# Two weight loads of a two-layer decode kernel are split unevenly over the DMA engines, head 29's keys are kept and loaded in another cut, and the small tasks move behind the values

## The chip, the core and the metric

The kernel runs on one core of a Trainium2 chip. TensorE (PE in the profile) multiplies matrices, VectorE (DVE), ScalarE (ACT) and GpSimd (POOL) work on vectors, SyncE (SP) issues transfers, and sixteen DMA engines move data from the chip's memory into the core's on-chip memory of 128 partitions. SP, ACT and POOL can each issue DMAs. The metric is the device time of one execution in microseconds, as the median of several runs: 1347.92 us before the change (three runs, 1347.71 to 1348.05).

## The reference

Two attention blocks and two MLP blocks run in turn over one token, and the two attention blocks use the same cache and the same weights, as the two MLP blocks do.

```python
def _A_ref(x, k_cache, v_cache, wq, wo):      # x: 1 x 1 x 640, caches: 32 heads x 8192 x 128
    q = heads of (x @ wq)
    scores = einsum("bhqd,bhkd->bhqk", q, k_cache) * (128 ** -0.5)
    p = softmax(scores)
    o = einsum("bhqk,bhkd->bhqd", p, v_cache)
    return o @ wo
def _B_ref(x, w1, w2):                        # 640 -> 1728 -> 640
    return relu(x @ w1) @ w2

x = A_x
x = x + _A_ref(_layernorm(x), A_k_cache, A_v_cache, A_wq, A_wo)
x = x + _B_ref(_layernorm(x), B_w1, B_w2)
x = x + _A_ref(_layernorm(x), ...)            # the same caches and weights again
x = x + _B_ref(_layernorm(x), ...)
```

All data are float32. The keys and values of one head are 8.39 MB, those of all heads 268 MB. They don't fit on the chip, so most of them are read twice, once in each layer.

## The kernel before

**The order of the work.** Layer 0 takes the heads from 0 to 31 and layer 1 from 31 to 0, so that what lies on the chip at the turn is used again. `kept` names the units that stay: the last units of head 29, the last of head 30 and all of head 31. Sizes are counted in places; a place is 8 floats in each of the 128 partitions, which is 4,096 bytes over all of them. `KEPT` is the number of places that stay, 3960 before the change. Keys and values go into one buffer, `ring`, of `KEPT + 800` places.

**Loads.** `todo` is the list of all loads in their order. `pump` (line 210) takes the first one, looks for a free place for it (`place`, or a fixed slot for the heads 2 to 26, which are called `FULL`) and issues it on SP's queue (line 230). If there is no room it returns and tries again at the next `release`, which follows the matmuls that read a piece (`scores`, line 509; `values`, line 564). A load of the ring has one row in each of the 128 partitions, so each of the sixteen engines carries eight rows of it, and the load has landed when the last of the sixteen has done its rows. The heads 27 to 31 are cut into units (`UNITS`), and each unit is one load. At the turn three loads go beside the ring, into `mix` and `wct` (`load_beside`, line 240), as soon as the tiles are free, and a `None` in `todo` holds SP until then. The program gives the DMAs that SP and ACT issue eight completion semaphores in turn; a DMA is issued when the one that had its semaphore eight DMAs before has landed.

**Weights.** The query weights and the output weights come in groups of four heads. A group is 10,240 bytes in a partition. They go into `pair` and are issued by ACT (`load_wq` line 278, `load_pair` lines 284 and 288). In layer 1 the second group's query weights are issued at the layer's start (line 729) and first read by `queries_by_halves` (line 434) beside the second head. Twelve of W2's fourteen row blocks come through the ring at the end of each layer; the last two (`w2_t`, `F_REST`) are loaded once, in layer 0 by ACT (line 809), as 128 rows of 5,120 bytes. Only 64 rows of the second of these blocks hold weights; the other 64 are zeros that nothing reads.

**Small tasks.** `chores` and `slow` are queues of generators: the output projection of a group (`run_out`), the next group's queries, and the product of W1 with the last head's output weights (`mixing`, `mixing_quarter`), which is made once in each layer. `side_work` advances them. In the `FULL` heads it runs twice between the exponentials and the values; in the other heads between the pieces of the keys and values. `keep_busy` issues matmuls whose result nobody reads, in layer 1 also beside the values of the last head but one.

**Ends.** A layer's last head (31 in layer 0, 0 in layer 1) comes in small pieces. After its last keys land there follow its scores, exponentials, values, the MLP and the layer's sum; in layer 1 the output is then stored.

Of the kernel before, what the change touches and what calls it, by code (L numbers as in the profile page):

```python
# [105 lines left out]
def decode_kernel(ctx: ExitStack, tc: tile.TileContext, x, kv, wqo, w1, w2, w2_rest, out):  # L106
# [16 lines left out]
    apart = {(29, 9): (3800, KEPT), (30, 0): (4464, 4544), (30, 1): (4544, RING), (30, 2): (3072, 3800)}  # L123
# [4 lines left out]
    def all_of(layer, u):  # L128
        todo.append((layer, u, 0, len(UNITS[u[0]][u[1]][1]), None))
# [8 lines left out]
    def turning(layer, heads, slot):  # L138

        for h in heads:  # L140
            for a, end in parts_of(layer, h):
                while a < end:
                    b = min(end, a + SLOTS - slot)
                    todo.append((layer, (h, 0), a, b, SLOT * slot))
                    slot = (slot + b - a) % SLOTS
                    a = b

    def anywhere(layer, h):
        for a, b in parts_of(layer, h):
            todo.append((layer, (h, 0), a, b, None))  # L150
# [21 lines left out]
    for u in W2_ALL:  # L172
        all_of(1, u)
# [36 lines left out]
    def pump():  # L210
        while todo:
# [17 lines left out]
            o = 8 * sum(ns[:first])  # L229
            nc.sync.dma_start(ring[:, 8 * at : 8 * (at + n)], source[u][:, o : o + 8 * n])  # L230
# [904 lines left out]
```

## Time and profile before

| | |
|---|---|
| median of three runs | 1347.92 us (1347.71 to 1348.05) |
| the profiled execution's own time | 1347.7 us |
| its span, first to last instruction | 1345.6 us |
| PE busy | 816.0 us, 61% of the span |
| DVE busy | 248.2 us, 18% |
| ACT busy | 58.6 us, 4% |
| POOL busy | 2.9 us, ten instructions |
| moved by DMA | 574.17 MB, mean 427 GB/s |
| mean granted TensorE clock | 0.807 |

How it is read: the slices and windows give the busy share of the sixteen DMA engines (1.00 is all of them) and the rate. A share above 1 comes where an engine has two packets under way. The chain of waits goes back from the last instruction to what released it at each step. In the list of waits, "SPq L230 <- X" is time in which SP's queue held a load back until X had happened.

### The profile page before, as it was taken

The numbers are of one execution on the slowest core, as the hardware profiler recorded it, in microseconds if no ns is written. First come the engines' busy times: TensorE is split into PE (matmuls) and PEld (weight loads), VectorE is DVE, ScalarE is ACT, GpSimd is POOL, SyncE is SP. The second block draws the span as 40 slices with busy tenths as digits, with TensorE's granted clock in tenths as the row PEclk, the third lists the DMA queues.
The fourth block names the chain that finished last, engine by engine and source line by source line (L and its number), as shares of the span: only waits on it lengthen the run. The fifth ranks groups of instructions, "written<-read, shape, count | busy, mean of one in ns | idle before, by whom it ended". The sixth has DMA issues, their size and how long they took to land.

```text
span 1345.6 us, 13351 instructions
## 1 busy us (share of the span) xinstructions
PE 816.0 (61%) x5968; PEld 264.3 (20%) x5968; DVE 248.2 (18%) x774; ACT 58.6 (4%) x149; POOL 2.9 (0%) x10
## 2 busy tenths in 40 slices
PE   3454565564655655667688754475456554666778
PEld 1111111111211211112252111111112111211224
DVE  1121111221211211112223211122111111111222
ACT  0000000000000000000000000000000000000000
POOL 0000000000000000000000000000000000000000
PEclk9688677887977977777899767787878788777789
DMA  9999999999999999999999999999999999999997
GB/s 406 437 427 438 429 429 433 428 434 431 442 429 426 434 436 420 440 423 412 423 409 425 432 436 432 428 435 433 433 435 425 425 433 436 429 427 449 416 426 329
DMA packets 22672, 574.17 MB, mean 427 GB/s; under 512 B 2516, under 2 KB 2648, under 8 KB 5592
## 3 DMA queue, kind: packets, MB, share of 16 engines
q1 hardware_dynamic: 19592, 529.84, 91.8%
q10 hardware_dynamic: 3024, 43.50, 7.6%
q8 instruction: 46, 0.75, 0.2%
q14 instruction: 10, 0.08, 0.0%
HBM read 573.33 MB, written 0.00 MB: 426 GB/s over the span
## 4 chain that ended last, share of the span: by engine, by line
DMA 61%; PE 29%; DVE 6%; ACT 1%; issue 1%; another core or an unknown queue 1%; SPq 0%; ACTq 0%; DVEq 0%
DMA ring<-in_kv 60%; PE ps L509 14%; PE outs L564 9%; DVE h_t L520 2%; DVE pt L538 1%; ACT p L534 1%; PE acc L478 1%; DMA pair<-in_wqo 1%; PE pm L525 1%; DVE p L601 1%; PE px L434 1%; PE px L466 1%; PE px L685 1%; DVE pT L540 0%
## 5 line engine op out<-in xcount | busy, mean ns | idle before, releaser
L509 PE MATMUL ps<-ring,spread_q 128*32 128x512 f32 (+3 forms) x2104 | 329.1, 775 | 295.2 <-DMA ring<-in_kv 290.3
L564 PE MATMUL outs<-ring,pT 128*4 128x512 f32 (+1 forms) x2032 | 272.3, 674 | 47.1 <-DVE pT L540 24.0
L509 PEld LDWEIGHTS ps<-ring,spread_q 128*32 128x32 f32 x2104 | 78.5, 138 | 480.2 <-issue 335.4
L520 DVE TENSOR_REDUCE h_t<-ps 128x1 f32<-128x512 f32 x64 | 44.2, 691 | 599.8 <-PE ps L509 599.8
L534 ACT ACTIVATE p<-ps,h_t 128x512 f32<-128x512 f32 x64 | 44.0, 687 | 1222.5 <-DVE h_t L532 1222.5
L564 PEld LDWEIGHTS outs<-ring,pT 128*4 128x4 f32 x2032 | 53.3, 93 | 218.1 <-issue 177.2
L611 PE MATMUL pm<-ones,p 128*128 128x1 f32 x120 | 22.9, 260 | 95.0 <-DVE p L601 95.0
L597 DVE TENSOR_SCALAR p<-outs,ind 128x128 f32<-128x128 f32 x60 | 21.0, 351 | 279.0 <-PE outs L564 279.0
L601 DVE SCALAR_TENSOR_TENSOR p<-outs,ind,p 128x128 f32<-128x128 f32 x180 | 63.1, 351 | 6.4
L538 DVE STREAM_TRANSPOSE pt<-p 128x512 f32<-128x512 f32 x64 | 46.5, 727 | 58.2 <-ACT p L534 58.2
L525 PE MATMUL pm<-row_of,h_t 128*128 128x16 f32 x128 | 25.9, 278 | 49.7 <-DVE h_t L520 48.9
L611 PEld LDWEIGHTS pm<-ones,p 128*128 128x128 f32 x120 | 17.8, 188 | 152.2 <-DVE p L601 150.9
L525 PEld LDWEIGHTS pm<-row_of,h_t 128*128 128x128 f32 x128 | 19.6, 192 | 110.0 <-DVE h_t L520 108.3
L434 PE MATMUL px<-pair,ln_xc 128*32 128x256 f32 x280 | 36.6, 412 | 4.2 <-ACT mix L693 4.2
L685 PE MATMUL px<-w_t,wct 128*128 128x448 f32 (+1 forms) x80 | 35.9, 563 | 1.0 <-ACT wct L678 1.0
L478 PE MATMUL acc<-pair,o_cols 128*32 128x320 f32 x224 | 36.3, 471 | 0.0
L434 PEld LDWEIGHTS px<-pair,ln_xc 128*32 128x32 f32 x280 | 16.3, 117 | 23.2 <-ACT mix L693 8.9
L532 DVE TENSOR_REDUCE h_t<-pm 128x1 f32<-128x16 f32 x64 | 11.2, 174 | 32.6 <-PE pm L525 32.6
L478 PEld LDWEIGHTS acc<-pair,o_cols 128*32 128x32 f32 x224 | 12.9, 118 | 17.4 <-issue 16.6
L685 PEld LDWEIGHTS px<-w_t,wct 128*128 128x128 f32 x80 | 13.5, 193 | 10.2 <-issue 8.6
L540 DVE COPY pT<-pt 128x64 f32<-128x64 f32 x64 | 14.3, 224 | 2.2
L615 DVE COPY o_cols<-pm 128x1 f32<-128x1 f32 x56 | 8.9, 158 | 28.4 <-PE pm L611 28.4
(136 smaller groups left out, 215.4 us busy)
## 6 DMA issues: line engine op xcount, KB each, us to landing
ring<-in_kv SPq DMA_DIRECT2D x24, 4096.0 KB, 32.1
ring<-in_kv SPq DMA_DIRECT2D x11, 6144.0 KB, 33.6
ring<-in_kv SPq DMA_DIRECT2D x31, 2048.0 KB, 30.6
pair<-in_wqo ACTq DMA_DIRECT2D x13, 2560.0 KB, 24.5
ring<-in_kv SPq DMA_DIRECT2D x14, 1024.0 KB, 11.9
ring<-in_w SPq DMA_DIRECT2D x4, 1280.0 KB, 25.9
w_t<-in_w ACTq DMA_DIRECT2D x1, 4320.0 KB, 29.0
ring<-in_kv SPq DMA_DIRECT2D x6, 512.0 KB, 28.3
```

What stands on the lines that cost most here:

```text
L434: nc.tensor.matmul(pq[32 * j : 32 * j + 32, :n], xc[:, c : c + 1].to_broadcast([P, 32]), wq_t[g][:, c, j * n : (j + 1) * n], start=(c == 0 ...
L478: nc.tensor.matmul(acc[32 * half : 32 * half + 32, : 2 * DR], col.to_broadcast([P, 32]), wt[:, 2 * half * DR : 2 * (half + 1) * DR], start ...
L509: nc.tensor.matmul(hd.ps[32 * g : 32 * g + 32, c : c + n], spread_q[:, 3 - r : 35 - r], tile_of[:, at + g * n : at + (g + 1) * n], start=f ...
L520: nc.vector.tensor_reduce(hd.nm, hd.ps, AX.X, ALU.max, negate=True)
L525: nc.tensor.matmul(pt[:, :16], hd.nm.to_broadcast([P, P]), row_of.rearrange("p g r -> p (g r)"), start=True, stop=True,)
L534: nc.scalar.activation(hd.p, hd.ps, AF.Exp, bias=hd.low, scale=1.0, accum_out=hd.l)
L538: nc.vector.transpose(pt, hd.p)
L564: nc.tensor.matmul(hd.out[32 * g : 32 * g + 4, r : r + m].rearrange("p r d -> p (r d)"), hd.pT[:, 4 * i : 4 * i + 4], tile_of[:, v : v + m ...
L597: nc.vector.tensor_scalar(oc[:, 0], hd.out[:, 0], ind[:, :1], 0.0, op0=ALU.mult, op1=ALU.add)
L601: nc.vector.scalar_tensor_tensor(oc[:, r], hd.out[:, r], ind[:, r : r + 1], oc[:, r - 1], op0=ALU.mult, op1=ALU.add,)
L611: nc.tensor.matmul(pt[:, :1], oc[:, 3], ones, start=True, stop=True)
L685: nc.tensor.matmul(pt[:, :n], wct[:, c], w1_t[:, c, f : f + n], start=(c == 0), stop=(c == NB - 1),)
```

## The change

- **Kept keys and the cut of head 29.** The last key piece of head 29 that stays grows from 320 to 416 columns and there is no separate 128-column unit. `KEPT` rises by 48 places to 4008, and the ring with it.
- **Longer loads.** `ENDS` and `STARTS` write out the loads at the end of layer 0 and the start of layer 1, and a load may now cover several units, which lie beside each other in a row in memory (`ROWS`). There are 17 loads in place of 27 for the heads 27 to 31 in layer 0, and 11 in place of 15 in layer 1. In layer 0 all keys of head 29 now come ahead of its values.
- **Half of W2's last rows.** ACT loads only rows 64 to 127 of the first of the two blocks (2,560 bytes each). Rows 0 to 63 of both blocks (5,120 bytes each) come in three loads that GpSimd issues, as 2 x 3, 6 x 7 and 8 x 2 rows. The 64 rows of zeros are no longer loaded.
- **80 rows of a group's query weights.** In layer 1 ACT loads rows 80 to 127 of the second group's query weights, and GpSimd rows 0 to 79 as 2 x 2, 6 x 10 and 8 x 2 rows. For both, the source is padded (`_apart`) so that the outer dimension of a load stays 2, 6 or 8.
- **Small tasks.** In the `FULL` heads the PE steps of the small tasks now run after the values, beside the vector work of the head's output, and the others behind the output. The product with the last head's weights is started at head 8 (its load at head 7) and its quarters at heads 10, 14, 18 and 22. `totals` moves behind a head's output, `queries_by_halves` has one pause fewer, and the three `keep_busy` matmuls beside the last head but one run in layer 0 too.
- **Room.** The identity lies in the ring's tail and is made again in layer 1; several small tiles are merged, and GpSimd's scratch is halved.

```diff
...
@@ -47,13 +47,12 @@
     ("k", K_ALL[:1]),
     ("k", K_ALL[1:2]),
     ("k", [(2, 0, 256)]),
-    ("k", [(2, 256, 256), (3, 128, 64)]),
+    ("k", [(2, 256, 256), (3, 0, 96)]),
     ("v", V_ALL[:1]),
     ("v", V_ALL[1:2]),
-    ("k", [(3, 0, 128)]),
     ("v", V_ALL[2:3]),
     ("v", V_ALL[3:]),
-    ("k", [(3, 192, 320)]),
+    ("k", [(3, 96, 416)]),
 ]
...
@@ -61,12 +60,42 @@
...
 UNITS[31] = HALVES[:2] + LAST
-DROPPED = {29: 9, 30: 2}
-KEPT = 3960
+DROPPED = {29: 8, 30: 2}
+ROWS = [[(h, i) for i in range(len(UNITS[h]))] for h in range(29)]
+ROWS += [[(h, i) for i in range(len(UNITS[h]))] for h in (29, 30, 31)]
+ENDS = [
+    [(27, 0)],
+    [(27, 1)],
+    [(28, 0), (28, 1)],
+    [(28, 2), (28, 3)],
+    ROWS[29][:4],
+    [(29, 8)],
+    ROWS[29][4:8],
+    [(30, 0), (30, 1)],
+    [(30, 2)],
+    [(30, 3)],
+    [(30, 4)],
+] + [[u] for u in ROWS[31]]
+STARTS = [
+    [(29, 0)],
+    [(29, 1)],
+    [(29, 2)],
+    [(29, 3)],
+    ROWS[29][4:6],
+    ROWS[29][6:8],
+    ROWS[28][:2],
+    ROWS[28][2:3],
+    [(28, 3)],
+    [(27, 0)],
+    [(27, 1)],
+]
+KEPT = 4008
 W2_PLACES = 800
+W2_SPREAD = [(2, 3), (6, 7), (8, 2)]
+WQ_SPREAD = [(2, 2), (6, 10), (8, 2)]
 WIDE = 64
 MIX_BEHIND = 3
-MIX_AT = [12, 16, 20, 24]
+MIX_AT = [10, 14, 18, 22]
 AHEAD = 3
...
-    apart = {(29, 9): (3800, KEPT), (30, 0): (4464, 4544), (30, 1): (4544, RING), (30, 2): (3072, 3800)}
+    apart = {(29, 8): (3800, KEPT), (30, 0): (RING - 296, RING), (30, 2): (3072, 3800)}
...
-    def all_of(layer, u):
-        todo.append((layer, u, 0, len(UNITS[u[0]][u[1]][1]), None))
+    def all_of(layer, us):
+        todo.append((layer, [(u, t) for u in us for t in range(len(UNITS[u[0]][u[1]][1]))], None))
...
-    for h in range(FULL[-1] + 1, H):
-        for i in range(len(UNITS[h])):
-            all_of(0, (h, i))
-    for u in W2_ALL[:-1]:
-        all_of(0, u)
-    for h in range(H)[:FULL[-1]:-1]:
-        if h != 30:
-            for i in range(len(UNITS[h])):
-                if (h, i) == (29, 2):
-                    todo.append(None)
-                if (h, i) not in kept:
-                    all_of(1, (h, i))
+    for us in ENDS + [[u] for u in W2_ALL[:-1]]:
+        all_of(0, us)
+    for n, us in enumerate(STARTS):
+        if n == 2:
+            todo.append(None)
+        all_of(1, us)
...
-    for us, dram in ((order, kv), (W2_ALL, w2)):
-        o = 0
-        for u in us:
-            n = 8 * P * size(UNITS[u[0]][u[1]])
-            source[u] = dram[o : o + n].rearrange("(p m) -> p m", p=P)
-            o += n
+    o = 0
+    for row in ROWS:
+        n = 8 * sum(size(UNITS[h][i]) for h, i in row)
+        block = kv[o : o + P * n].rearrange("(p m) -> p m", p=P)
+        o += P * n
+        a = 0
+        for h, i in row:
+            source[h, i] = block, a
+            a += 8 * size(UNITS[h][i])
...
                 todo.pop(0)
...
-            layer, u, first, last, at = todo[0]
-            unit = UNITS[u[0]][u[1]]
-            ns = [wide(kind_of(unit, t), piece) for t, piece in enumerate(unit[1])]
-            n = sum(ns[first:last])
+            layer, pieces, at = todo[0]
+            ns = []
+            for u, t in pieces:
+                unit = UNITS[u[0]][u[1]]
+                ns.append(wide(kind_of(unit, t), unit[1][t]))
+            n = sum(ns)
             if at is None:
-                at = place(layer, u, n)
+                at = place(layer, pieces[0][0], n)
                 if at is None:
                     return
             elif not is_free(at, n):
                 return
             todo.pop(0)
-            o = 8 * sum(ns[:first])
-            nc.sync.dma_start(ring[:, 8 * at : 8 * (at + n)], source[u][:, o : o + 8 * n])
-            for t in range(first, last):
-                live[layer, u, t] = at, ns[t]
+            u, t = pieces[0]
+            block, o = source[u]
+            unit = UNITS[u[0]][u[1]]
+            o += 8 * sum(wide(kind_of(unit, i), unit[1][i]) for i in range(t))
+            nc.sync.dma_start(ring[:, 8 * at : 8 * (at + n)], block[:, o : o + 8 * n])
+            for (u, t), m in zip(pieces, ns):
+                live[layer, u, t] = at, m
                 at_of[layer, u, t] = ring, 8 * at
-                at += ns[t]
+                at += m
...
+
+    def load_spread(where, parts, rows):
+
+        a = 0
+        for i, (k, n) in enumerate(rows):
+            nc.gpsimd.dma_start(where[a : a + k * n], parts[i, :k, :n])
+            a += k * n
...
-    ones = consts.tile([P, 1], F32, name="ones")
+    small = consts.tile([P, 12], F32, name="small")
+    ones, mhalf, ind, sel = small[:, 0:1], small[:, 1:2], small[:, 2:7], small[:, 7:12]
...
-    ident = consts.tile([P, P], F32, name="ident")
+    ident = ring[:, 8 * SLOT * SLOTS : 8 * SLOT * SLOTS + P]
     make_identity(nc, ident)
...
-        row = work.tile([P, n], F32, name="q_row")
+        row = work.tile([P, RUN], F32, name="p")[:, :n]
         nc.vector.tensor_scalar(
             row[:64], pq[:64, :n], r[0][:64], SCALE, op0=ALU.mult, op1=ALU.mult
         )
-        yield "pe"
         pt = ps_m.tile([P, 512], F32, name="px")
...
         if L:
-            load_wq(groups[1], nc.scalar)
+            wq_t[groups[1]] = as_wq(1)
+            nc.scalar.dma_start(pair[80:, 1], wqo[chain(groups[1], 0)][80:, groups[1]])
+            load_spread(pair[:, 1], wq_last, WQ_SPREAD)
...
             if L == 0 and where == 7:
-                nc.scalar.dma_start(w2_t, w2_rest)
-            if where == 8:
+                nc.scalar.dma_start(w2_t[64:, 0], w2_rest)
+                load_spread(w2_t.rearrange("p f n -> p (f n)"), w2_last, W2_SPREAD)
+            if where == 7:
                 of, nth = divmod(last, HG)
                 if L:
+                    make_identity(nc, ident)
                     n = D // 8
                     assert is_free(RING - n, n)
                     live["last"] = RING - n, n
                 raw = ring[:, 8 * RING - D :] if L else mix[:, :D]
                 nc.scalar.dma_start(raw, wqo[chain(of, 1)][:, of, nth * D : (nth + 1) * D])
                 wo_last.append(raw if L else as_wo(0)[:, nth])
-            if where == 11:
+            if where == 8:
                 slow.append([mixing(wo_last[-1] if L else mix[:, :D]), "dve"])
             if where in MIX_AT:
...
-            else:
+            elif h not in FULL:
                 side_work()
-                if h in FULL:
...
-                totals(sums[k])
...
-                if L and near_end and a == 1:
+                if near_end and a == 1:
                     keep_busy(2)
             col = o_cols[k][:, j : j + 1]
             if near_end:
                 rows = copied_rows(hd)
-                if L:
-                    keep_busy(1, 256)
...
                 steps = output(hd, col, k == NG - 1)
                 next(steps)
+                if k < NG - 1 and j == HG - 1:
+                    totals(sums[k])
                 if after is not None:
                     pending = steps
+                elif h in FULL and (L or h < FULL[-1]):
+                    work_off("pe")
+                    at_once(steps)
+                    work_off("dve")
+                    side_work()
                 else:
                     at_once(steps)
                 if k < NG - 1 and j == HG - 1:
-                    nc.vector.tensor_tensor(o_cols[k], o_cols[k], sums[k][:, HG:], op=ALU.mult)
+                    nc.vector.tensor_tensor(o_cols[k], o_cols[k], sums[k][:, HG : 2 * HG], op=ALU.mult)
...
+def _apart(rows, spread):
+
+    n = max(n for _, n in spread) + 1
+    apart = np.zeros((len(spread), 8, n, rows.shape[1]), rows.dtype)
+    a = 0
+    for i, (k, m) in enumerate(spread):
+        apart[i, :k, :m] = rows[a : a + k * m].reshape(k, m, -1)
+        a += k * m
+    return apart
+
...
-    for h in range(H):
-        for unit in UNITS[h]:
-            n = 8 * size(unit)
...
-        "w2_rest": rows[:, 4 * F_TILES :],
+        "w2_rest": rows[64:, 4 * F_TILES],
+        "w2_last": _apart(rows[:64, 4 * F_TILES :].reshape(64, -1), W2_SPREAD),
+        "wq_last": _apart(wq[NG - 2], WQ_SPREAD),
...
     nc = bacc.Bacc(
-        "TRN2", target_bir_lowering=False, num_devices=1, dynamic_dma_scratch_size=1024
+        "TRN2", target_bir_lowering=False, num_devices=1, dynamic_dma_scratch_size=512
```

More of the change, by code (lines that the diff above doesn't have):

```diff
@@ L105, in decode_kernel @@
 @with_exitstack
-def decode_kernel(ctx: ExitStack, tc: tile.TileContext, x, kv, wqo, w1, w2, w2_rest, out):
+def decode_kernel(ctx: ExitStack, tc: tile.TileContext, x, kv, wqo, w1, w2, w2_rest, w2_last, wq_last, out):
     nc = tc.nc
@@ L143, in turning @@
                     b = min(end, a + SLOTS - slot)
-                    todo.append((layer, (h, 0), a, b, SLOT * slot))
+                    todo.append((layer, [((h, 0), t) for t in range(a, b)], SLOT * slot))
                     slot = (slot + b - a) % SLOTS
@@ L149, in anywhere @@
         for a, b in parts_of(layer, h):
-            todo.append((layer, (h, 0), a, b, None))
+            todo.append((layer, [((h, 0), t) for t in range(a, b)], None))
     for h in range(FULL[0]):
@@ L239, in load_beside @@
         assert 8 * size(UNITS[u[0]][u[1]]) == n
-        nc.sync.dma_start(where[:, at : at + n], source[u])
+        block, o = source[u]
+        nc.sync.dma_start(where[:, at : at + n], block[:, o : o + n])
         for t, piece in enumerate(pieces):
@@ L418, in queries @@
         yield "dve"
-        row = work.tile([P, 2 * DH], F32, name="q_row")[:, :DH]
+        row = work.tile([P, DR], F32, name="q_row")[:, :DH]
         nc.vector.tensor_scalar(row, pq[:, :DH], r[0], SCALE, op0=ALU.mult, op1=ALU.mult)
@@ L492, in __init__ @@
             self.ps = ps_s.tile([P, RUN], F32, name="ps")
-            t = work.tile([P, 4], F32, name="h_t", bufs=2)
-            self.nm, self.low = (t[:, i : i + 1] for i in range(2))
-            self.sums = sums
-            self.l, self.rl = sums[:, j : j + 1], sums[:, HG + j : HG + j + 1]
+            self.l, self.rl, self.nm, self.low = (
+                sums[:, HG * i + j : HG * i + j + 1] for i in range(4)
+            )
     def spread(h):
@@ L655, in mixing @@
         wc = mix[:, :D]
-        s = work.tile([P, 1], F32, name="m_s")
+        s = work.tile([P, 1], F32, name="ln_m")
         nc.vector.tensor_reduce(s, raw, AX.X, ALU.add)
@@ L798, in due @@
                 o_cols[k] = work.tile([P, HG], F32, name="o_cols", bufs=2)
-                sums[k] = work.tile([P, 2 * HG], F32, name="sums", bufs=2)
+                sums[k] = work.tile([P, 4 * HG], F32, name="sums", bufs=2)
             if where and j == 0:
@@ L889, in attention_and_mlp @@
                 rows = copied_rows(hd)
-                if L:
-                    keep_busy(1, 256)
+                keep_busy(1, 256)
                 summed_rows(hd, rows, col)
@@ L933, in attention_and_mlp @@
                 sums_of_rows(pt, rows, False, range(2))
-        o_late = work.tile([P, 2 * DH], F32, name="q_row")[:, :DH]
+        o_late = work.tile([P, DR], F32, name="q_row")[:, :DH]
         nc.vector.tensor_copy(o_late, late)
@@ L1076, in _laid_out @@
     o = 0
-    for h in range(H):
-        for unit in UNITS[h]:
-            n = 8 * size(unit)
-            block = kv[o : o + P * n].reshape(P, n)
-            o += P * n
-            a = 0
+    for row in ROWS:
+        n = 8 * sum(size(UNITS[h][i]) for h, i in row)
+        block = kv[o : o + P * n].reshape(P, n)
+        o += P * n
+        a = 0
+        for h, i in row:
+            unit = UNITS[h][i]
             for t, piece in enumerate(unit[1]):
```

16 lines of the change are left out of this document (8 added, 8 removed).

## The prediction

> **What bounds the kernel now.** I read the page first: its slices, queues and chain of waits.
>
> ```profile
> span 1345.6 us, 13351 instructions
> DMA  9999999999999999999999999999999999999997
> q1 hardware_dynamic: 19592, 529.84, 91.8%
> q10 hardware_dynamic: 3024, 43.50, 7.6%
> q8 instruction: 46, 0.75, 0.2%
> DMA 61%; PE 29%; DVE 6%; ACT 1%; issue 1%; another core or an unknown queue 1%; SPq 0%; ACTq 0%; DVEq 0%
> ```
>
> All sixteen DMA engines work from the first slice to the last. The transfers set the time, and a saved byte counts if it is saved on the engine that ends last. The loads of SP (queue 1) and ACT (queue 10) give every engine the same rows. Queue 8 is different: 46 packets, 0.2% of 16 x 1345.6 us, so about 0.9 us of one engine each. Sixteen engines would get 2.7 us of them in the whole run, eight would get 5.4. The windows at the end show which it is; the last two columns are the share of the engines and the rate.
>
> ```profile
> 1335.50:1336.00 0.50, 0.40 (x7) 0.29 (x3) 0.35 (x2) 0.31 (x2) 0.00 (x0) 1.00 1.04 430
> 1336.00:1336.50 0.50, 0.50 (x6) 0.45 (x5) 0.26 (x2) 0.05 (x1) 0.00 (x0) 1.00 0.86 358
> 1336.50:1337.00 0.50, 0.50 (x17) 0.42 (x16) 0.23 (x2) 0.00 (x0) 0.00 (x0) 1.00 0.69 287
> 1337.00:1337.50 0.50, 0.50 (x19) 0.29 (x15) 0.00 (x0) 0.00 (x0) 0.00 (x0) 1.00 0.54 225
> 1338.00:1338.50 0.50, 0.50 (x24) 0.43 (x14) 0.00 (x0) 0.00 (x0) 0.00 (x0) 1.00 0.54 225
> 1339.00:1339.50 0.50, 0.50 (x17) 0.16 (x9) 0.00 (x0) 0.00 (x0) 0.00 (x0) 1.00 0.53 197
> 1340.50:1341.00 0.50, 0.49 (x14) 0.17 (x4) 0.28 (x2) 0.00 (x0) 0.00 (x0) 1.00 0.10 41
> ```
>
> The engines don't end together. Some six stop between 1336 and 1337, one or two a little later, and then 0.54 of the sixteen, eight or so, work until 1339 to 1341. So there is an early half, 4 to 5 us ahead, and a late half, which fits refills on eight engines only. The end waits for the late half:
>
> ```profile
> 639.90 11.94 DMA ring<-in_kv
> 651.88 1.34 PE ps L509 x8
> 656.75 1.93 PE outs L564 x8
> 658.70 22.55 DMA ring<-in_kv
> 681.30 1.97 PE ps L509 x16
> 1292.31 29.98 DMA ring<-in_kv
> 1322.34 1.97 PE ps L509 x16
> 1342.59 0.38 DVE xr L1041
> ```
>
> Each layer ends with the landing of its last keys, which is that of the slowest engine (681.3 and 1322.3), and a fixed string of PE and DVE work, here 20.6 us to the layer's sum. An engine's own loads ahead of those keys therefore move the end one for one.
>
> **The change part by part.** The price of a row comes from the rates:
>
> ```profile
> 20.00:340.00 320.00, 167.32 (x1104) 47.97 (x1100) 52.69 (x154) 11.74 (x30) 0.00 (x0) 0.76 1.00 432
> 612.00:626.00 14.00, 9.76 (x59) 2.36 (x53) 3.69 (x12) 0.78 (x2) 0.00 (x0) 0.78 1.00 423
> 1293.00:1321.00 28.00, 24.28 (x182) 8.54 (x186) 4.94 (x17) 1.15 (x3) 0.00 (x0) 0.88 1.00 426
> ```
>
> 426/16 is 26.6 GB/s for an engine: 0.385 us for a row of 10,240 bytes, 0.192 for 5,120.
>
> *Kept keys.* 48 places are 196,608 bytes, 12,288 on each engine: -0.46 us, early in layer 1.
>
> *W2's last rows.* Before, each engine had 8 x 5,120 = 40,960 bytes. Now each has four rows of 2,560 from ACT, and besides two of 5,120 (eight engines: 20,480 in all, -0.77 us), three (two engines: -0.58) or seven (six engines: 46,080, +0.19). 10,240 bytes an engine, 0.38 us, are the zeros left out; the rest is moved.
>
> *Query weights.* Before, eight rows of 10,240 on each engine. Now three from ACT and two from GpSimd on ten engines (-3 rows, -1.15 us), three and ten on six engines (+5 rows, +1.92).
>
> Which engines these are no trace here shows; that each GpSimd load runs on as many as its outer dimension, and the three on different ones, is an assumption. For it speaks the shape of the split, eight light, two between and six heavy, beside an end in which eight are late and some six early. [...]
>
> *Longer loads.* 14 fewer loads on SP, about 25.5 MB in longer rows. At 423 GB/s that takes 60.3 us, at 432 it takes 59.0: between nothing and -1.3, and I take half, -0.6, since the rows become 26 to 33 KB and not 64. In layer 0 they do more:
>
> ```profile
> 637.00:638.00 1.00, 1.00 (x9) 0.15 (x4) 0.00 (x0) 0.00 (x0) 0.00 (x0) 0.50 0.67 276
> 638.00:639.00 1.00, 1.00 (x12) 0.24 (x8) 0.00 (x0) 0.00 (x0) 0.00 (x0) 0.63 0.81 272
> SPq L230 <- DMA pair<-in_wqo: 11.2, 1, 11.2
> ```
>
> SP stood 11.2 us behind a load of ACT whose semaphore it needed, and at 637 part of the engines ran dry. Fewer and longer loads put more bytes into the eight that may be under way. I count nothing for it: 276 of 427 GB/s say that ten engines went on, and those are the late ones.
>
> *GpSimd's issues.* POOL's program has nothing else there. Its three loads wait, as ACT's did, for the first queries' matmuls:
>
> ```profile
> 705.32 0.33 ACTq L278 DMA_DIRECT2D pair<-in_wqo  x1
> 707.78 1.99 SPq L230 DMA_DIRECT2D ring<-in_kv  x3
> 726.00 2.11 PE L434 MATMUL px<-pair,ln_xc 128*32 128x256 f32 x18
> pair<-in_wqo ACTq DMA_DIRECT2D x2, 1280.0 KB, 9.4
> L338 POOL TENSOR_TENSOR ln_r<-ln_v,mhalf 128x1 f32<-128x1 f32 x4 | 2.2, 550 | 1338.6 <-DVE ln_v L336 1338.6
> ```
>
> Eight rows landed 9.4 us after the issue; thirteen need between 13 x 0.385 = 5.0 and 9.4 x 13/8 = 15.3, so until 720.6 at most, and PE reads them at 726.0. The issues lie beside the loads under way. Another price is possible: the light engines have three rows less to do while SP's next loads, now fewer, come at 707.8; if they run dry, up to 1.15 comes back. I take 0.2 of 0 to 1.15, since four loads were issued just before.
>
> *Order and small tasks.* Head 29's last keys come ahead of 4.19 MB of its values (9.8 us), so what PE and DVE did from 651.88 to 656.75 is done by then. That makes room for the added `keep_busy` in layer 0:
>
> ```profile
> 1311.41 2.31 PE L400 MATMUL px<-w_t 128*128 128x512 f32 x4
> 1315.48 0.70 PE L400 MATMUL px<-w_t 128*128 128x256 f32 x2
> 681.30 1.92 PE L509 MATMUL ps<-ring,spread_q 128*32 128x512 f32 x16 [0.72 <-DMA ring<-in_kv]
> mix<-in_wqo ACTq DMA_DIRECT2D x1, 320.0 KB, 23.6
> ```
>
> They cost 3.0 us of PE; PE waited 0.72 for the last keys and gains 4.9, so nothing; without that cover it is 3.0 - 0.7 = +2.3. The tasks that move behind the values of the `FULL` heads lie where PE waits for the next keys: nothing. The last head's weights are now read at the end of the head after the one that issues them, nearly two heads of 8.39 MB (39 us) against 23.6 to land: nothing. The identity made again is work on an idle POOL: nothing.
>
> *The sum* for the late eight, against the profiled execution's 1347.7 (span 1345.6 and 2.1 around it; 0.2 under the median): -0.46 - 0.77 - 1.15 - 0.6 + 0.2 = -2.8, so **1344.9 us**. The six heavy ones lose 3.07 of their lead of 4 to 5 us in layer 1 (1.92 + 1.15) and stay ahead; what is late next is the same half.
>
> **The rivals.**
>
> *The heavy rows fall on late engines* (slower). If one of the six is of the late half, its terms are -0.46 + 0.19 + 1.92 - 0.6 = +1.05: **1348.8**. It decides from a lead under 3.07 us on. For it: no view names an engine. Against it: the counts eight and six.
>
> *The split does nothing.* GpSimd's rows go evenly over sixteen engines: four rows of W2 and eight of query weights each. Left are the bytes not moved and the longer loads, -0.46 - 0.38 - 0.6 = -1.4: **1346.3**. [...]
>
> *Cover gone.* Light engines run dry at layer 1's start (+1.0 more) or `keep_busy` delays layer 0's last keys (up to +2.3): **1345.9 to 1347.2**. For it: SP's issue at 707.78, the slack of 0.72. Against it: the 4.9 us.
>
> *The weights come late* (slower). If GpSimd's rows land after 726.0, PE stops, releases nothing, and SP's loads follow late. With some 8 us of loads queued, it costs from about 734 on, and to lose all the gain and 2.7 more they must land near 740, 34 us after the issue against 9.4: **1350.6** and over.
>
> *More than counted.* Longer loads at 1.3, nothing lost at layer 1's start and an end evened out by 0.5: **1343.7**.
>
> **How the numbers follow.** Forecast 0.52 (1344.1 to 1345.7), more than counted 0.12, split without effect 0.12, cover gone 0.12, heavy on late engines 0.07, late weights 0.05. The range 1343.7 to 1347.2 holds the first four but for their edges, some 0.8. A change of 0.2%, 2.7 us, is what a measurement can tell from none: below 1345.2 lies about two thirds of the forecast's own range and the case of more, 0.46; above 1350.6 only the last, 0.05; the rest 0.49.
>
> **What would show it.** Right: the share at the end falls from 1.00 to 0.1 in about 3 us instead of 5, the last keys land some 1.2 us earlier in layer 0 and 2.8 in layer 1, no dip near 637, and the string behind the last keys keeps its 20.6 us. Wrong: an end in which six engines work after the others (the heavy are late); an end as long as before (no split); a wait of PE at line 434 for `pair`; shares under 1 between 705 and 720; a wait shorter than 0.7 us ahead of layer 0's last keys. What I can't see, and what would undo it, is the place of GpSimd's rows.

## The result, and the profile after

The changed kernel takes **1357.37 us** (median of six runs, 1356.54 to 1358.64) against 1347.72 for the kernel before beside it: ratio 1.0072, 95% interval 1.0062 to 1.0083. It is slower by some 9.7 us. Forecast were 1344.9, range 1343.7 to 1347.2; the prediction was wrong, and in sign. The profiled execution took 1358.26 us, its span is 1356.4.

In the page, the sixteen engines are as busy as before, but two slices in the middle move less than the rest, and GpSimd's queue is new:

```profile
DMA  9999999999999999999999999999999999999997
GB/s 404 419 425 432 441 414 433 425 430 435 435 433 423 440 435 423 430 432 427 424 382 353 436 430 433 427 442 431 424 412 431 428 429 429 443 416 447 417 428 324
q1 hardware_dynamic: 17576, 529.64, 91.4%
q10 hardware_dynamic: 2880, 42.19, 7.5%
q0 software_dynamic: 512, 1.15, 0.4%
```

The chain of waits, from the last keys of layer 0 to those of layer 1 (start, length, what):

```profile
650.87 32.55 DMA ring<-in_kv
683.46 1.97 PE ps L549 x16
703.63 13.88 DMA mix<-in_kv
717.55 0.93 PE ps L549 x8
721.98 24.56 DMA ring<-in_kv
1300.42 32.68 DMA ring<-in_kv
1333.14 1.97 PE ps L549 x16
```

Layer 0's last keys land at 683.4 and not at 681.3: 2.2 us are lost by then. Layer 1's land at 1333.1 and not at 1322.3: 10.8 are lost, so 8.6 of them in layer 1. The row at 703.63 is new: head 30's keys in `mix`, which were there in time before, took 13.9 us to land, and PE waited 0.8 us for them.

The windows show where it happens (length, busy time of PE, PE's weight load, DVE, ACT, POOL, clock, share of the DMA engines, GB/s):

```profile
637.00:638.00 1.00, 0.56 (x6) 0.38 (x10) 0.84 (x4) 0.00 (x0) 0.00 (x0) 0.50 1.00 421
700.00:710.00 10.00, 8.95 (x150) 5.97 (x146) 2.76 (x17) 0.00 (x0) 2.82 (x5) 1.00 0.99 373
710.00:715.00 5.00, 4.10 (x39) 1.13 (x35) 0.95 (x3) 0.08 (x1) 0.00 (x0) 1.00 1.08 207
715.00:720.00 5.00, 4.19 (x56) 1.35 (x52) 1.64 (x3) 0.69 (x2) 0.00 (x0) 1.00 1.02 229
720.00:730.00 10.00, 7.95 (x84) 2.85 (x80) 2.76 (x9) 0.78 (x2) 0.28 (x2) 0.83 1.00 360
```

From 710 to 720 the engines are all busy (1.08 and 1.02) and move 207 and 229 GB/s, half of the 420 of before. They are not idle; their packets are slow. The same stretch of the kernel before, for comparison:

```profile
710.00:715.00 5.00, 4.08 (x54) 1.52 (x54) 1.90 (x5) 0.78 (x2) 0.00 (x0) 1.00 1.01 420
715.00:720.00 5.00, 3.77 (x44) 0.96 (x36) 1.75 (x5) 0.00 (x0) 0.00 (x0) 1.00 1.03 420
```

The DMA view of 710 to 713 (packets, MB, share of 16 engines x 3 us) tells how slow, before GpSimd's rows have begun:

```profile
q10 hardware_dynamic: 43, 0.44, 84.7%
q1 hardware_dynamic: 88, 0.32, 30.1%
q0 software_dynamic: 3, 0.00, 0.2%
```

84.7% of 48 us is 40.7 us for 0.44 MB, which is 43 rows of 10,240 bytes: 0.95 us for a row of ACT's, where the prediction had 0.385. In the kernel before, from 706 to 712, ACT's 0.95 MB took 37.5% of 96 us, which is 0.39 us for a row. The landings follow (KB, us from issue to landing):

```profile
mix<-in_kv SPq DMA_DIRECT2D x1, 864.0 KB, 13.9
pair<-in_wq_last POOLq DMA_DIRECT2D x1, 600.0 KB, 19.1
pair<-in_wqo ACTq DMA_DIRECT2D x1, 480.0 KB, 10.3
pair<-in_wq_last POOLq DMA_DIRECT2D x1, 160.0 KB, 19.9
```

### The profile page after: what moved, and what is told of

The parts are those of the page before. It is cut to its first block, busy times and chain, and to the rows that moved or that the text cites. A ratio compares the mean times of both kernels' runs of the same rounds, so it can differ in the third digit from the quotient of the medians.

```text
span 1356.4 us, 13343 instructions
## 1 busy us (share of the span) xinstructions
PE 832.6 (61%) x5958; PEld 261.9 (19%) x5958; DVE 247.0 (18%) x774; ACT 59.1 (4%) x149; POOL 7.0 (1%) x18
## 3 DMA queue, kind: packets, MB, share of 16 engines
q0 software_dynamic: 512, 1.15, 0.4%
## 4 chain that ended last, share of the span: by engine, by line
DMA 64%; PE 26%; DVE 6%; ACT 2%; issue 1%; another core or an unknown queue 1%; SPq 0%; ACTq 0%; DVEq 0%
DMA ring<-in_kv 62%; PE ps L549 12%; PE outs L604 10%; DVE pt L578 2%; DVE sums L560 2%; ACT p L574 2%; DMA pair<-in_wqo 1%; PE pm L565 1%; DMA mix<-in_kv 1%; DVE p L641 1%; PE px L507 1%; PE acc L519 1%; DVE pT L580 1%; DVE sums L572 0%
## 5 line engine op out<-in xcount | busy, mean ns | idle before, releaser
L549 PE MATMUL ps<-ring,spread_q 128*32 128x512 f32 (+4 forms) x2088 | 311.9, 744 | 266.8 <-DMA ring<-in_kv 263.5
L604 PE MATMUL outs<-ring,pT 128*4 128x512 f32 (+1 forms) x2032 | 308.8, 761 | 136.8 <-DVE pT L580 107.0
L560 DVE TENSOR_REDUCE sums<-ps 128x1 f32<-128x512 f32 x64 | 44.2, 691 | 559.0 <-PE ps L549 559.0
L574 ACT ACTIVATE p<-ps,sums 128x512 f32<-128x512 f32 x64 | 44.0, 687 | 1155.5 <-DVE sums L572 1155.5
L637 DVE TENSOR_SCALAR p<-outs,small 128x128 f32<-128x128 f32 x60 | 21.0, 351 | 314.6 <-PE outs L604 314.6
L641 DVE SCALAR_TENSOR_TENSOR p<-outs,small,p 128x128 f32<-128x128 f32 x180 | 63.1, 351 | 6.4
L565 PE MATMUL pm<-row_of,sums 128*128 128x16 f32 x128 | 25.9, 278 | 49.6 <-DVE sums L560 48.9
L651 PE MATMUL pm<-small,p 128*128 128x1 f32 x120 | 22.3, 255 | 38.1 <-DVE p L641 24.9
L565 PEld LDWEIGHTS pm<-row_of,sums 128*128 128x128 f32 x128 | 19.6, 193 | 107.9 <-DVE sums L560 106.2
L651 PEld LDWEIGHTS pm<-small,p 128*128 128x128 f32 x120 | 18.7, 190 | 72.3 <-DVE p L641 43.0
L476 PEld LDWEIGHTS px<-pair,ln_xc 128*32 128x32 f32 x280 | 16.1, 110 | 22.0 <-issue 10.8
```

Of the source, the lines that this page charges most:

```text
L476: nc.tensor.matmul(pq[32 * j : 32 * j + 32, :n], xc[:, c : c + 1].to_broadcast([P, 32]), wq_t[g][:, c, j * n : (j + 1) * n], start=(c == 0 ...
L549: nc.tensor.matmul(hd.ps[32 * g : 32 * g + 32, c : c + n], spread_q[:, 3 - r : 35 - r], tile_of[:, at + g * n : at + (g + 1) * n], start=f ...
L560: nc.vector.tensor_reduce(hd.nm, hd.ps, AX.X, ALU.max, negate=True)
L565: nc.tensor.matmul(pt[:, :16], hd.nm.to_broadcast([P, P]), row_of.rearrange("p g r -> p (g r)"), start=True, stop=True,)
L574: nc.scalar.activation(hd.p, hd.ps, AF.Exp, bias=hd.low, scale=1.0, accum_out=hd.l)
L604: nc.tensor.matmul(hd.out[32 * g : 32 * g + 4, r : r + m].rearrange("p r d -> p (r d)"), hd.pT[:, 4 * i : 4 * i + 4], tile_of[:, v : v + m ...
```

## The experiments

The theories, as the expectations name them. **A**: GpSimd's way of issuing loads is slow. **B**: the merged loads and the new order starve SP's queue. **C**: uneven rows, more on some engines than on others, hold the rest up. **D**, formed after the first four runs: a load that reaches only a part of the 128 partitions has several engines writing into the same few, and they hold each other up. Each ratio is to the kernel before, measured beside the run. How many rows one of GpSimd's loads puts on an engine is the prediction's assumption throughout, and that engines meet in the same partitions is D's explanation: no trace names an engine. What is measured are times, shares, rates and packets. The diffs show the lines that matter; arguments and host arrays that go with them are left out.

| run | what it is | median us | ratio, 95% interval |
|---|---|---|---|
| 1 | query weights whole by ACT | 1349.85 | 1.0019 (1.0009 to 1.0028) |
| 2 | W2's rows whole by ACT | 1353.29 | 1.0043 (1.0028 to 1.0058) |
| 3 | both by ACT | 1346.02 | 0.9988 (0.9978 to 0.9997) |
| 4 | the small loads by ACT | 1360.56 | 1.0096 (1.0079 to 1.0114) |
| 5 | as 3, weights in halves of the rows | 1351.46 | 1.0029 (1.0020 to 1.0038) |
| 6 | as 3, weights in halves of the columns | 1347.24 | 0.9999 (0.9989 to 1.0009) |
| 7 | as 2, split by columns | 1350.10 | 1.0019 (1.0010 to 1.0029) |
| 8 | as 3, weights whole by GpSimd | 1347.08 | 0.9998 (0.9988 to 1.0008) |
| 9 | as 3, W2's rows whole by GpSimd | 1347.63 | 0.9997 (0.9988 to 1.0006) |
| 10 | as 1, W2's 128 rows as 2, 6 and 8 | 1351.16 | 1.0023 (1.0013 to 1.0034) |
| 11 | as 3, W2 in two loads of 64 rows | 1349.86 | 1.0020 (1.0012 to 1.0028) |
| 12 | as 3, the longer loads taken apart | 1348.61 | 1.0005 (0.9997 to 1.0014) |
| 13 | as 3, weights cut at row 80, even | 1352.57 | 1.0037 (1.0023 to 1.0051) |
| 14 | run 3 again | 1346.18 | 0.9992 (0.9983 to 1.0000) |

### Which part of the change costs (runs 1 to 4)

These four start from the changed kernel. Run 1:

```diff
-            nc.scalar.dma_start(pair[80:, 1], wqo[chain(groups[1], 0)][80:, groups[1]])
-            load_spread(pair[:, 1], wq_last, WQ_SPREAD)
+            load_wq(groups[1], nc.scalar)
```

> The changed kernel, except that ACT again loads all 128 rows of the second group's query weights in layer 1 (1.31 MB, as before the change). Theory A, GpSimd's load at the start of layer 1 is the cause: in the changed kernel's trace the sixteen engines lose 9.2 us between 690 and 730 (1.56 + 1.04 + 5.25 + 1.31, elapsed time less the work moved), 1.2 in the same stretch before; with ACT's load the 8 us come back and the light engines carry 1.15 more: about 1357.4 - 8 + 1.2 = 1350.5. Rival B, the merged loads and the new order starve SP's queue there: the loss stays and the light engines do 1.15 more: 1358.5. Rival C, uneven rows on the engines: as A in this run; the fourth run of this call tells it from A.

Run 2:

```diff
-                nc.scalar.dma_start(w2_t[64:, 0], w2_rest)
-                load_spread(w2_t.rearrange("p f n -> p (f n)"), w2_last, W2_SPREAD)
+                nc.scalar.dma_start(w2_t, w2_rest)
```

> The changed kernel, except that ACT again loads W2's last 128 rows whole (0.66 MB with the zeros, at head 7). GpSimd's three loads for them were issued at 10.3 us in the changed kernel, and the engines lose 3.1 us between 20 and 200 us, against 0.2 before. Theory A (GpSimd's loads cost on their own): these 2.9 come back, the late engines carry 0.77 more: 1357.4 - 2.9 + 0.8 = 1355.3, and layer 0's last keys land near 681.3 and not 683.5. Rival B (order and merged loads): nothing comes back, 1358.2.

Run 3 has both edits.

> The changed kernel with both of GpSimd's loads given back to ACT: what is left of the change is kept keys, the cut and order of head 29, longer loads, and the moved small tasks. Theory A: 1357.4 - 8 + 1.2 - 2.9 + 0.8 = 1348.5, at most; the prediction's own terms for these parts give 1347.7 - 0.46 - 0.6 = 1346.6. Rival B, these parts are what costs: 1355 and over.

Run 4 changes only the queue:

```diff
-            nc.gpsimd.dma_start(where[a : a + k * n], parts[i, :k, :n])
+            nc.scalar.dma_start(where[a : a + k * n], parts[i, :k, :n])
```

> The changed kernel, with the six small loads (2, 6 and 8 rows outermost) issued by ACT and not by GpSimd; rows, sizes and places in memory are unchanged. Theory A, it is GpSimd's way of issuing that costs: the losses at 20 to 200 and 690 to 730 go, and if ACT's loads fall on the same engines 1346 or less is measured; if they don't, about 1347 to 1348. Rival C, the uneven rows themselves hold the other loads up: as long as the changed kernel, 1357. Four loads at the start of layer 1 in place of one also take four of the eight semaphores that SP and ACT share; that could cost up to some 5 us.

Taking back the query weights' split gives 7.5 us, W2's 4.1, both 11.4 in medians and 1.0072 - 0.9988 = 0.0084 (11.3 us) in ratios: they add up. Theory A's 1350.5 for run 1 was near; its 1355.3 for run 2 was not (1353.29), W2's rows cost twice what it had. Rival B falls: without the splits the merged loads and the order are no slower than the kernel before. In run 3's windows the dip is gone:

```profile
700.00:710.00 10.00, 8.15 (x106) 4.13 (x94) 2.54 (x12) 0.00 (x0) 0.55 (x1) 1.00 1.02 404
710.00:715.00 5.00, 4.92 (x62) 1.83 (x66) 1.84 (x5) 0.78 (x2) 0.00 (x0) 1.00 1.02 429
715.00:720.00 5.00, 3.20 (x44) 0.83 (x32) 1.48 (x5) 0.00 (x0) 0.00 (x0) 1.00 1.00 423
720.00:730.00 10.00, 9.17 (x96) 4.05 (x96) 2.61 (x7) 0.78 (x2) 0.50 (x2) 1.00 1.03 444
```

Run 2, which keeps the split of the query weights, has the dip, while PE does as much from 710 to 715 as it did before (4.11 us busy; 4.08 before), and its chain has no wait for `mix`. So PE's short wait for `mix` in the changed kernel is a result of the slow packets, and not their cause:

```profile
710.00:715.00 5.00, 4.11 (x54) 1.51 (x54) 1.90 (x5) 0.78 (x2) 0.00 (x0) 1.00 0.99 188
715.00:720.00 5.00, 3.63 (x44) 0.96 (x36) 1.89 (x5) 0.00 (x0) 0.00 (x0) 1.00 1.02 278
```

Run 4 was expected near 1347 by theory A and is the slowest of all, with the dip and without GpSimd, here from its windows:

```profile
710.00:715.00 5.00, 4.10 (x42) 1.18 (x38) 0.91 (x3) 0.00 (x0) 0.00 (x0) 1.00 1.04 148
715.00:720.00 5.00, 5.00 (x64) 1.54 (x60) 1.68 (x4) 0.78 (x2) 0.00 (x0) 1.00 1.02 239
```

Run 4 also moves W2's small loads, from 10 us to where ACT's queue comes to them (166.5 us in run 3); and its loads share their semaphores with SP's, which its expectation priced at up to some 5 us (in the changed kernel SP waited 7.3 us for a load of `pair`). The engines were at a share of 1.04 and 1.02 in the dip.

Theory A isn't refuted by this alone: the three loads may lie on other engines in run 4 than in the changed kernel, and no trace here names an engine. What the runs show of it is the small packets of ACT's loads: one whole load more adds 16 packets under 512 B (2,292 in run 3, 2,308 in run 5 below), and the six small loads of run 4 add 32 in all (2,324), as 2, 6 and 8 engines twice would if each adds one. But a dip of the same kind with no load of GpSimd's asked for another cause. ACT's 48 rows were slow before GpSimd's first came, and 48 can be three for each of sixteen engines, so they need not be uneven. What sets them apart from a whole load is where they go: partitions 80 to 127.

### What makes the packets slow (runs 5 to 8)

All four keep W2 on ACT. Runs 5, 6 and 8 start from run 3, run 7 from run 2. Run 5:

```diff
-            load_wq(groups[1], nc.scalar)
+            wq_t[groups[1]] = as_wq(1)
+            for a in (64, 0):
+                nc.scalar.dma_start(pair[a : a + 64, 1], wqo[chain(groups[1], 0)][a : a + 64, groups[1]])
```

> The kernel of the third run (1346.0 us: both loads on ACT), except that ACT loads the second group's query weights in layer 1 in two loads, rows 64 to 127 and then rows 0 to 63. Every engine carries the same bytes as there, four rows of each load, and GpSimd issues nothing. Theory D: what costs is that a load reaches only a part of the 128 partitions, so that several engines write into the same eighth of them and hold each other up (in the changed kernel ACT's rows for partitions 80 to 127 took 2.9 to 3.9 times their 0.385 us before GpSimd's first row came). Then rows of these loads take about 0.8 us and the 1.31 MB take some 6 us at about 215 GB/s in place of 3.1, with SP's rows held up behind them: 1349 to 1353, with a dip in the rate at 705 to 720. Rivals A and C (GpSimd's way of issuing; uneven engines): no dip, 1346.

Run 6 has the same two loads by columns:

```diff
+            for a in (1280, 0):
+                nc.scalar.dma_start(pair[:, 1, a : a + 1280], wqo[chain(groups[1], 0)][:, groups[1], a : a + 1280])
```

> The third run's kernel, except that ACT loads the same query weights in two loads by columns: the second half of all 128 rows and then the first (5,120 bytes of each row). As many loads, bytes and semaphores as the run beside it, but each load reaches all 128 partitions. Theory D: 1346, no dip. If a second load at the start of layer 1 is what costs: as the run with halves of the rows.

Run 7:

```diff
-WQ_SPREAD = [(2, 2), (6, 10), (8, 2)]
+WQ_SPREAD = [(2, 6), (6, 14), (8, 4)]
-            nc.scalar.dma_start(pair[80:, 1], wqo[chain(groups[1], 0)][80:, groups[1]])
-            load_spread(pair[:, 1], wq_last, WQ_SPREAD)
+            nc.scalar.dma_start(pair[:, 1, :1280], wqo[chain(groups[1], 0)][:, groups[1], :1280])
+            load_spread(pair[:, 1, 1280:], wq_last, WQ_SPREAD)
```

> The second run's kernel (1353.3: W2 on ACT, the query weights split), except that the split is by columns: ACT loads the first half of all 128 rows, GpSimd the second half (5,120 bytes each) as 2 x 6, 6 x 14 and 8 x 4 rows. Eight engines so carry 8 x 5,120 and 4 x 5,120 bytes, the six 8 and 14: the same lead of the light engines, 2 rows of 10,240 less than in the third run (-0.77). Theory D: most of the dip goes, since ACT's half reaches all partitions and GpSimd's rows are spread over them; 1345.3 to 1348. Rival C, that uneven engines hold the others up: still 1352 to 1354, with a dip as before. Rival A, GpSimd's issuing: the same 1352 to 1354.

Run 8:

```diff
-            load_wq(groups[1], nc.scalar)
+            load_wq(groups[1], nc.gpsimd)
```

> The third run's kernel, except that GpSimd and not ACT issues the second group's query weights in layer 1, whole, as one load of 128 rows. All engines carry eight rows of it, as in ACT's load. Theory D: no dip, 1346 to 1347 (the rows start some 5 us after the issue, as they did in the changed kernel, which is early enough for 726). Rival A, GpSimd's way of issuing is what costs: 1351 to 1353.

Runs 5 and 6 differ in which partitions one load reaches, and with it in the length of a row, 10,240 bytes against 5,120. The length isn't the cause: rows of 10,240 bytes took 0.39 us in the kernel before. Halves of the rows cost 1.0029 - 0.9988, 5.5 us against run 3; halves of the columns 1.5, inside their intervals. The DMA view of 708 to 714, first run 5 and then run 6:

```profile
DMA packets 188, 1.30 MB, mean 217 GB/s; under 512 B 30, under 2 KB 30, under 8 KB 88
q10 hardware_dynamic: 122, 1.02, 82.5%
q1 hardware_dynamic: 66, 0.28, 20.6%
```

```profile
DMA packets 518, 2.55 MB, mean 424 GB/s; under 512 B 60, under 2 KB 60, under 8 KB 501
q10 hardware_dynamic: 281, 1.29, 52.2%
q1 hardware_dynamic: 237, 1.26, 51.0%
```

ACT's rows take 82.5% of 16 x 6 us for 1.02 MB in run 5, 0.80 us for 10,240 bytes, and 52.2% for 1.29 MB in run 6, 0.40 us. SP's rows beside them (queue 1) slow down too: 71 us of an engine for a MB in run 5, 39 in run 6. The whole core moves 217 and 424 GB/s. Half of the partitions, half of the rate: run 5 comes out as theory D has it, and neither uneven engines nor GpSimd's issuing is in it. (That its loads are even is read from the 16 small packets that the second one adds.) A cut by rows also changes which rows of memory one load reads. No run separates reading from writing; that W2's rows, from another array, are slowed in the same way (run 11) speaks for the partitions.

The changed kernel's 207 GB/s at 710 to 715, where ACT's rows go to partitions 80 to 127, are near the 217 of run 5. Both are rates of the whole core, with SP's rows in them; ACT's rows of run 5 alone, sixteen engines at 0.80 us each, make 205. Why rows slow down when their load reaches a part of the partitions is not shown: no trace tells which engine writes to which partitions.

Run 8 settles theory A. GpSimd's one load of 128 rows was issued at 704.72, landed 8.6 us later (ACT's in run 3 needed 9.1), and there is no dip; 1347.08 is at the upper end of D's 1346 to 1347:

```profile
710.00:715.00 5.00, 4.68 (x58) 1.73 (x62) 1.89 (x6) 0.78 (x2) 0.00 (x0) 1.00 1.05 436
pair<-in_wqo POOLq DMA_DIRECT2D x1, 1280.0 KB, 8.6
```

Run 7 was expected at 1345.3 to 1348 by D, and took 1350.1: better than run 2 (1353.3), worse than run 6 by 0.0020, 2.7 us. All partitions are reached by the loads together and it still dips, less deep:

```profile
710.00:715.00 5.00, 4.11 (x42) 1.15 (x38) 1.10 (x4) 0.78 (x2) 0.00 (x0) 1.00 1.06 343
715.00:720.00 5.00, 5.00 (x72) 1.58 (x64) 1.50 (x3) 0.00 (x0) 0.00 (x0) 1.00 1.03 309
```

So run 5's form of D isn't all. The uneven rows of theory C may be the rest; no run isolates that, and why they would slow the others down is not shown. Three rivals are untested. Each of GpSimd's loads in run 7 alone reaches only 12, 84 or 32 partitions, so the cost of run 5 may be in it too. GpSimd's split rows come with many packets under 512 B (see runs 9 and 10). And a heavy engine has, by the prediction's assumption, six rows of 5,120 bytes more, 1.2 us at 0.192 each, which would count without any slow packet if that engine is a late one.

### W2's rows, and the longer loads (runs 9 to 12)

Runs 9, 11 and 12 start from run 3. Run 9:

```diff
-                nc.scalar.dma_start(w2_t, w2_rest)
+                nc.gpsimd.dma_start(w2_t, w2_rest)
```

> The third run's kernel (both loads on ACT), except that GpSimd issues W2's last 128 rows in one load; POOL waits for nothing there, so it goes out near 10 us and not at head 7. [...] Theory D (rows that reach a part of the partitions, or that an engine writes where another one writes, hold each other up): the same as the third run, 1346 to 1347. If GpSimd's early issue beside the first loads is what cost 3.8 us in the changed kernel: 1349 to 1350.

Run 10, from run 1 (W2's zeros are loaded again, so that all 128 rows take part):

```diff
-W2_SPREAD = [(2, 3), (6, 7), (8, 2)]
+W2_SPREAD = [(2, 6), (6, 14), (8, 4)]
-                nc.scalar.dma_start(w2_t[64:, 0], w2_rest)
```

> As the run beside it, but GpSimd brings the same 128 rows as 2 x 6, 6 x 14 and 8 x 4 rows. All 128 partitions are reached, the engines carry 4, 6 or 14 rows in place of 8. If uneven engines could pay: 4 rows of 5,120 bytes less on the late eight, 1346.0 - 0.8 = 1345.2. [...]

Run 11:

```diff
-                nc.scalar.dma_start(w2_t, w2_rest)
+                nc.scalar.dma_start(w2_t[64:, 0], w2_rest[64:, 0])
+                nc.scalar.dma_start(w2_t[:64], w2_rest[:64])
```

> The third run's kernel, except that ACT loads W2's last rows in two loads of 64 rows without the zeros (2,560 and 5,120 bytes a row: 0.49 MB in place of 0.66). Bytes alone: -0.38, 1345.6. Theory D: each of the two loads reaches half of the partitions, 215 GB/s as in the run with halves of the rows, so 2.3 us in place of 1.55, +0.75 and as much again where SP's rows are held up: 1346.5 to 1348.

Run 12:

```diff
-    for us in ENDS + [[u] for u in W2_ALL[:-1]]:
+    ends = [[u] for row in ENDS for u in row if u[0] < 30] + [us for us in ENDS if us[0][0] >= 30]
+    for us in ends + [[u] for u in W2_ALL[:-1]]:
...
-    for n, us in enumerate(STARTS):
+    for n, us in enumerate([[u] for row in STARTS for u in row]):
```

> The third run's kernel with its longer loads taken apart, in the same order: one load for each unit of the heads 28 and 29 in layer 0 and in layer 1's start (eight and three loads more). What is left of the change is kept keys, the order of head 29 and the moved small tasks. The prediction's term for longer loads was -0.6 of 0 to -1.3: 1346.6 (1346 to 1347.3). If they are worth nothing: 1346.0; if fewer loads under way hold SP back at layer 1's start (SP waits there for releases), taking them apart gains: 1345.

In the changed kernel and in runs 9 and 10 GpSimd issues W2's rows at 10 us, since POOL has nothing to wait for there. That isn't the cost: run 9 does so with whole rows and is at 0.9997, 1.2 us over run 3 (1347.63, a little over D's 1346 to 1347). Cut into 2, 6 and 8 (run 10) it is 3.5 us slower than run 9, and 1351.16 is far from the 1345.2 of uneven engines that pay. The profiled execution of run 10, 1353.35 us, was its slowest. The DMA view of 20 to 100 us, run 9 and then run 10:

```profile
DMA packets 1005, 34.56 MB, mean 432 GB/s; under 512 B 112, under 2 KB 112, under 8 KB 185
```

```profile
DMA packets 1240, 33.25 MB, mean 416 GB/s; under 512 B 345, under 2 KB 345, under 8 KB 466
```

1.31 MB less, which is 3.1 us at 427 GB/s. Run 10 has 233 packets under 512 B more; by their own time they are little, since all of GpSimd's queue takes 2.2% of the engines' time there (1.1% in run 9), and whether they cost otherwise is not shown. Run 11 has even engines (by the small packets, 2,308 as in run 5), fewer bytes and no load of GpSimd's, and is 4.3 us slower than run 3, more than D's 0.5 to 2. The DMA view of 180 to 200 us, run 11 and then run 3, shows why:

```profile
DMA packets 244, 7.29 MB, mean 365 GB/s; under 512 B 48, under 2 KB 48, under 8 KB 138
q1 hardware_dynamic: 121, 6.88, 91.8%
```

```profile
DMA packets 288, 8.89 MB, mean 444 GB/s; under 512 B 32, under 2 KB 32, under 8 KB 160
q1 hardware_dynamic: 144, 8.39, 96.8%
```

1.60 MB less, 3.7 us. SP's own rows are the slow ones: 91.8% of 320 us for 6.88 MB is 42.7 us for a MB, against 36.9. ACT's second load, 0.33 MB, is on its way beside SP's rows of up to 65,536 bytes until 199.5 us (issue 168.5, landing 31.0 later); that engines meet in the same partitions for that long would be D's explanation. The price isn't that of the rows that are cut; it is paid by SP's rows while they are under way.

Run 12 puts the longer loads at 0.0013 to 0.0017 by the two measurements of run 3, 1.8 to 2.3 us with intervals of over a microsecond on each side; its 1348.61 is over the 1346 to 1347.3 that was expected. The prediction's -0.6 has the right sign and is small; that fewer loads starve SP, so that taking them apart gains, is refuted.

### The cut alone, and what is left (runs 13 and 14)

Run 13, from run 3, in place of `load_wq`:

```diff
+            for a, b, queue in ((80, P, nc.scalar), (0, 80, nc.gpsimd)):
+                queue.dma_start(pair[a:b, 1], wqo[chain(groups[1], 0)][a:b, groups[1]])
```

> The third run's kernel, except that the second group's query weights in layer 1 are cut as in the change, rows 80 to 127 by ACT and rows 0 to 79 by GpSimd, but GpSimd brings its 80 rows in one load, five on each engine, so that every engine carries 3 + 5 rows as in the whole load. If the part of the partitions that a load reaches is what costs (theory D), this cut alone takes most of the 7.3 us that the split cost: 1350 to 1353. If it is the unevenness alone: 1346 to 1347. If both add up, as the halves of the rows (+4.2 to 5.4) and the split by columns (+2.9) make it look: 1349.5 to 1351.

Run 14 is run 3's kernel.

> The third run's kernel once more, both loads on ACT, nothing else undone: kept keys, the cut and order of head 29, longer loads and the moved small tasks. It gave 1346.0, 0.9988 of the kernel before with an interval from 0.9978 to 0.9997. If that holds: 0.9980 to 0.9995, 1345.0 to 1347.0. The prediction's terms for these parts make 0.9992 (-1.06). If the first measurement was luck: 1.000.

The cut at row 80, with five and three rows on every engine by its expectation, costs 1.0037 - 0.9992, 6.1 us, nearly all of the 7.3 that the split into 2, 6 and 8 cost. By 720 it has recovered further than run 2:

```profile
710.00:715.00 5.00, 4.10 (x58) 1.63 (x58) 1.90 (x5) 0.78 (x2) 0.00 (x0) 1.00 0.97 213
715.00:720.00 5.00, 3.49 (x44) 0.86 (x32) 2.03 (x6) 0.00 (x0) 0.00 (x0) 1.00 1.03 384
```

So most of the price of the query weights' split is that of the cut by rows: about 6 us, where run 7's split by columns, which reaches all partitions together, costs 2.7, and the changed kernel's split 7.3. With intervals of nearly 2 us each way in runs 2 and 13, 7.3 and the sum of 8.8 can't be told apart, so whether the two prices add up stays open. The windows of 700 to 730 of run 13 sum to 11.1 MB and those of run 3 to 12.7, which is 3.8 us. The profiled executions of the two, 1350.41 and 1345.88, are 4.5 apart and not 6.1, so the dip holds most of that.

Run 14 gives 0.9992 again for the kernel without the splits, at most level with the kernel before at the upper end of its interval. It beats the changed kernel by 11 us and the kernel before by 1 to 1.6 in the two measurements. That is the version to keep.

## Why the prediction was wrong

- **What bounds the kernel**: right. The transfers set the time, and each layer ends with the landing of its last keys; the profile after shows the same two landings, 2.2 and 10.8 us later.
- **The price of a row: the step that failed.** "0.385 us for a row of 10,240 bytes" came from windows in which every load reached all 128 partitions. The terms for W2's last rows (-0.77) and the query weights (-1.15) multiplied it by the rows left on an engine, as if a row cost its engine the same wherever it goes. In the changed kernel ACT's rows cost 0.95 us from 710 to 713, and the rows beside them got dearer too, which the prediction put at nothing without a reason (in run 11 SP's took 42.7 us of an engine for a MB in place of 36.9). Measured, the two terms are +4.1 and +7.5.
- **Two, six and eight engines**: no run shows these counts for GpSimd's loads, and -0.77 and -1.15 rest on them; what the runs show in their place is +4.1 and +7.5. For ACT's loads, the small packets of run 4 fit the counts. Between 717 and 722 GpSimd's queue holds 26.3% of the engines' time, some four engines of sixteen, as rows left on a few heavy engines would. But what lead the six had was not spent without loss in any run: runs 7 and 10, whose loads together reach all partitions, cost 2.7 and 3.5 us, for the unevenness or for what comes with it.
- **GpSimd's issues**: the bound "until 720.6 at most" fell, since it scaled the 9.4 us of a whole load; the last rows landed near 729 (issued at 708.9, 19.9 us). PE read them at 730.8 and had no wait on them at that line. The term of 0.2 for light engines that run dry had its cause wrong too: at 710 to 720 the share is 1.02 to 1.08.
- **Longer loads** (-0.6): right in sign, measured about -2. **The dip at 637** is gone as the text said it would show (421 GB/s at a share of 1.00, against 276 at 0.67).
- **Order, kept keys and small tasks**: with run 12 at 1.0005 (0.9997 to 1.0014), nothing that can be measured; -0.46 for the kept keys is within it. The added `keep_busy` costs nothing that shows: in run 3 layer 0's last keys land at 680.1, 1.2 earlier than before, and layer 1's at 1320.4, 1.9 earlier.

```profile
680.14 1.97 PE ps L549 x16
1320.45 1.97 PE ps L549 x16
```

- **The end.** Forecast was a fall of the share in 3 us. It takes 5, and the plateau of 0.54 has become a slope (windows of the changed kernel). In run 3, without the splits, the plateau is still there (0.52 to 0.59 from 1336 to 1338), so the splits did move the ends of some engines:

```profile
1346.50:1347.00 0.50, 0.49 (x4) 0.49 (x5) 0.17 (x2) 0.36 (x2) 0.00 (x0) 1.00 0.85 348
1348.50:1349.00 0.50, 0.50 (x24) 0.50 (x20) 0.20 (x2) 0.00 (x0) 0.00 (x0) 1.00 0.47 195
1350.50:1351.00 0.50, 0.50 (x14) 0.47 (x17) 0.24 (x2) 0.00 (x0) 0.00 (x0) 1.00 0.15 61
```

- **The rivals.** "The weights come late" (1350.6 and over, 0.05) had the right sign and place, but not the mechanism: the price is paid by slow packets and not by a wait of PE for the weights. "The split does nothing" (1346.3) was 11 us under the 1357.4 that came; it too took the split for harmless, and 1346.0 was measured only without it (run 3). "The heavy rows fall on late engines" (+1.05) had the sign, but no view names an engine, and it is a ninth of what was lost. ("More than counted" adds up to 1343.5 by the prediction's own terms, not 1343.7, and so does the lower edge of the range.) No rival had a row that gets dearer by how its load is cut, and the range was bounded by rows of whole loads only.

## What to carry to other kernels

The price of a row, 0.39 us for 10,240 bytes, was measured on loads that reach all 128 partitions; it was 0.80 in loads of 64 rows and 0.95 in one of 48. Cut a load by columns, not by rows (+1.5 and +5.5 us here), and if it must be cut by rows, take the price of its rows from such a load, and count the other transfers under way beside it too (SP's rows took 42.7 us for a MB in place of 36.9). Relieving some engines by giving their rows to others did not pay here in any form tried, by rows with GpSimd or ACT or by columns with GpSimd; for the forms that reach all partitions the reason is not settled. A busy share of 1.00 with half the rate is the sign of it (1.08 and 207 GB/s at 710 to 715): read the share and the rate of a window together.

## What the hardware showed that was not expected

- Two loads of 64 rows moved 217 GB/s on a core that moves 424 with two loads of half the columns, bytes, queue and number of loads being the same.
- 0.49 MB in such loads cost 3.7 us of transfers, since SP's rows beside them took 42.7 us for a MB in place of 36.9 for as long as they were under way.
- A load issued by GpSimd was as good as one by ACT (8.6 and 9.1 us to land 1.31 MB).
- The same six small loads on ACT's queue were not better but worse, 1360.6 against 1357.4. No run shows on which engines they fall; waits for the semaphores that ACT and SP share are another reading.
